# Handing one gate-weight load from SyncE's queue to ScalarE's in a GeGLU feed-forward kernel

## The chip, the core and the metric

The kernel runs on one core of a Trainium2 chip. The metric is the device time of one execution, in microseconds; the kernel before was run six times, and the median is what the change is measured against. One further execution was taken with the hardware profiler. Its trace supplies every duration of a single instruction or transfer below; times inside it are counted in us from the span's start.

## The reference

```python
# x (32, 32, 1024), w_gate and w_up (1024, 3584), w_down (3584, 1024), all bf16
def reference(x, w_gate, w_up, w_down):
    return (gelu_tanh(x @ w_gate) * (x @ w_up)) @ w_down
```

The 32 x 32 rows of x are flattened to 1024 tokens. Two matrix products over the 1024 features give gate and up, each 1024 x 3584; the gated product is multiplied by w_down.

## The kernel before, in words

**Tiles.** Features, 1024 of them, lie in 8 contraction blocks of 128, called k = 0 to 7. The 3584 hidden columns are 28 tiles of 128, called m. Tokens come in two halves of 512. For the first product TensorE holds a 128 x 128 block of a weight matrix and streams 512 tokens of x, with the features on the partitions, so x has to be transposed: `xT[0]` holds half 0, `xT[1]` half 1. The index j is 0 for the gate weights and 1 for the up weights. `first` holds the weights of tiles m = 0 to 3 (512 columns) for both j and all k. It lies in the same SBUF arena as `xT`, so the profile calls all of them `arena`.

**The program.** Every operation is put down with `pr.add(engine, ...)`, which derives its waits from the memory cells that it reads and writes. `finish` sorts the list of each engine but TensorE's by the time given as `at`, and, where that is equal, by the order in which the operations were added. `emit` then writes them out; every instruction therefore shows line 117 in the profile. All loads in the opening have `at=0`, so there the order of adding is the order on each queue. A DMA is issued by the sequencer of SyncE (called SPq in the profile) or of ScalarE (ACTq), and each of the two has a hardware queue of its own: q1 for SyncE, q10 for ScalarE.

**The opening, in the order of the two issuing queues.** First each of them loads half of a small piece of x, blocks k = 0 and 1 of token half 0 (`xn`), which TensorE transposes and DVE copies to `xT[0]`. Blocks k = 2 to 7 of that half are transposed on the way in, by five DMA transposes from SyncE (`load_x`): one each for k = 2, 3, 4 and 5, and a double one for k = 6 and 7. The weights come through `load_first(eng, j, k0, k1)`, 128 KB for one j and one k.

| queue | before: issued in the opening, in order |
| --- | --- |
| SyncE | xn (half), gate k=0, gate k=1, transposes k=2, 3, 4, 5, 6-7 |
| ScalarE | xn (half), up k=0, up k=1, gate k=2, up k=2, gate k=3, up k=3, table load and warm-up Gelu |

Behind that, ScalarE issues four loads of 256 KB that wait for TensorE: gate and up of k = 4-5 after the last matmul of k = 0 (m = 3, j = 1), and gate and up of k = 6-7 after the last matmul of k = 1. SyncE's next load waits for the last matmul of k = 3 (`begin_late`).

**The first stage of matmuls.** After eight warm-up matmuls and the eight transposes of `xn`, TensorE runs `steps`: for each k from 0 to 5, the four tiles m with j = 0 and then the four with j = 1. So 32 matmuls of 128x512 use k = 0 to 3, and the next four need gate k=4, the four after that up k=4. At k = 3 every PSUM bank is copied out into `kept` (ScalarE for even m, DVE for odd m) for later use, and the k = 4 matmul of a bank has to come after that copy. After this stage, TensorE goes on through the rest of the kernel, a Strassen-like scheme over the 2 x 2 blocks of both products, in an order written out by hand.

Of the kernel before, what the change touches and what calls it, by code (L numbers as in the profile page):

```python
# [123 lines left out]
def bass_standalone__geglu_ffn__sampling_kernel(  # L124
# [21 lines left out]
    with ExitStack() as es:  # L146
# [42 lines left out]
        def dma(eng, out, a, at, name, after=()):  # L189
            return pr.add(eng, "dma_start", out, a, at=at, dma=name, after=after)  # L190
# [12 lines left out]
        NX = 2  # L203
# [3 lines left out]
        def load_first(eng, j, k0, k1, after=()):  # L207
            dma(eng, first[:, j, k0:k1, :], w_r[j][:, k0:k1, 0:4 * P], 0, f"w0_{j}_{k0}", after)
# [2 lines left out]
            pr.add("sp", "dma_start_transpose", xT[h][:, k0:k1, :], xf[h * 512:(h + 1) * 512, k0 * P:k1 * P],  # L211
                   dma=f"x{k0}_{h}", after=after)

        for k in range(NX):
            load_first("sp", 0, k, k + 1)
            load_first("act", 1, k, k + 1)
        for k0, k1 in ((2, 3), (3, 4), (4, 5), (5, 6), (6, 8)):
            load_x(0, k0, k1)
        for k in range(2, 4):
# [403 lines left out]
```

## Time and profile before

| | before |
| --- | --- |
| median of 6 runs | 273.14 us (272.87 to 273.6) |
| the profiled execution's own time | 274.18 us |
| its span, first to last instruction | 272.1 us |
| TensorE busy | 268.8 us, 99% of the span |
| DVE, ScalarE, GpSimd busy | 75%, 49%, 14% |
| granted TensorE clock | 1.00 |
| moved by DMA | 27.46 MB, mean 101 GB/s |

How to read it: the profiled execution lies 1.04 us above the median and has 2.1 us around its span, so a difference is worked out within the trace and then put on the median. "Busy" is the time in which an engine has an instruction under way; DMA issue is not counted as busy. A line of the timeline gives start, length, engine, operation, how many were merged, and in brackets the idle time ahead of it and what ended that. "To landing" is the time from the start of the issuing instruction to the last semaphore count of the transfer.

### The profile page before, as it was taken

Reading aid. Unit: us, or ns where it says so; the run is one execution under the profiler, and the core shown is the slowest. Engines: PE = TensorE matmul, PEld = TensorE weight load, DVE = VectorE, ACT = ScalarE, POOL = GpSimd, SP = SyncE. Lnnn points to the kernel's source line nnn. Section 1 sums busy time; section 2 is a strip of 40 time slices with the busy share of each in tenths; the row PEclk is TensorE's granted clock in tenths of the full one; section 3 lists DMA queues with packets and bytes.
Section 4 is the critical chain, followed back from the end, with each engine's and each line's share of the span. In section 5 each row is a group of like instructions: output and inputs, shape, how many; then the busy total and the mean of one; then the engine's idle time right before and its main releaser. Section 6 shows DMA issues by size and latency. Waiting matters only on the chain.

```text
span 272.1 us, 3323 instructions
## 1 busy us (share of the span) xinstructions
PE 268.8 (99%) x1206; PEld 191.6 (70%) x1206; DVE 203.3 (75%) x238; ACT 133.1 (49%) x213; POOL 37.1 (14%) x23
## 2 busy tenths in 40 slices
PE   8999999999999999999999999999999999999996
PEld 3444438888888888888776776674458888888884
DVE  1332997998898889888855738379976999999911
ACT  2335677566756675667455564531220305067452
POOL 1000003033303330333354160000000000000000
PEclk9999999999999999999999999999999999999999
DMA  7999970050393500851900071194010000002102
GB/s 165 235 297 222 285 186 4 1 154 0 94 292 78 148 6 2 255 170 40 272 0 0 0 239 33 60 348 136 0 39 19 4 0 0 0 0 80 58 19 96
DMA packets 47039, 27.46 MB, mean 101 GB/s; under 512 B 8624, under 2 KB 47024, under 8 KB 47024
## 3 DMA queue, kind: packets, MB, share of 16 engines
q1 hardware_dynamic: 44800, 25.30, 34.6%
q10 hardware_dynamic: 2224, 1.97, 3.1%
q8 instruction: 9, 0.15, 0.2%
q14 instruction: 6, 0.05, 0.1%
HBM read 23.33 MB, written 2.10 MB: 93 GB/s over the span
## 4 chain that ended last, share of the span: by engine, by line
PE 97%; DMA 2%; DVE 0%; issue 0%
PE ps L117 97%; DMA arena<-in_w_gate_dram 2%; DVE o L117 0%
## 5 line engine op out<-in xcount | busy, mean ns | idle before, releaser
L117 PE MATMUL ps<-S,T 128*128 128x512 f32 x560 | 129.2, 391 | 0.0
L117 PEld LDWEIGHTS ps<-S,T 128*128 128x128 f32 x560 | 105.1, 188 | 22.4
L117 ACT ACTIVATE tmp<-ps 128x512 f32<-128x512 f32 x64 | 38.1, 597 | 52.8 <-PE ps L117 52.8
L117 POOL TENSOR_TENSOR T<-arena 128x1024 fp32r<-128x1024 bf16 x17 | 36.4, 2152 | 125.4 <-PE ps L117 74.2
L117 PE MATMUL ps<-T,S 128*128 128x512 f32 x224 | 51.3, 390 | 0.0
L117 DVE TENSOR_TENSOR T<-arena,T 128x1024 fp32r<-128x1024 bf16 x42 | 50.9, 1217 | 0.2
L117 DVE TENSOR_TENSOR hT<-tmp,ps 128x512 bf16<-128x512 f32 x56 | 37.1, 684 | 14.9 <-PE ps L117 12.5
L117 PEld LDWEIGHTS ps<-T,S 128*128 128x128 f32 x224 | 42.0, 188 | 8.8
L117 PE MATMUL ps<-arena 128*128 128x512 bf16 x192 | 43.9, 385 | 0.4 <-DMA arena<-in_w_gate_dram 0.3
L117 ACT ACTIVATE ps<-ps 128x512 f32<-128x512 f32 x44 | 25.7, 585 | 36.6 <-PE ps L117 36.6
L117 DVE TENSOR_TENSOR tmp<-ps,tmp 128x512 f32<-128x512 f32 x28 | 19.4, 692 | 24.0 <-PE ps L117 23.8
L117 PEld LDWEIGHTS ps<-arena 128*128 128x128 bf16 x192 | 17.7, 99 | 25.2 <-issue 4.0
L117 DVE TENSOR_TENSOR T<-arena 128x1024 fp32r<-128x1024 bf16 x25 | 30.0, 1220 | 4.4 <-PE ps L117 4.4
L117 PE MATMUL ps<-arena,hT 128*128 128x512 bf16 (+2 forms) x126 | 24.6, 356 | 0.0
L117 DVE TENSOR_TENSOR ps<-ps,tmp 128x512 f32<-128x512 f32 x32 | 22.2, 695 | 3.0 <-PE ps L117 3.0
L117 PEld LDWEIGHTS ps<-arena,hT 128*128 128x128 bf16 x126 | 11.7, 98 | 12.7 <-issue 0.5
L117 ACT ACTIVATE tmp<-tmp 128x512 f32<-128x512 f32 x28 | 17.6, 634 | 2.4 <-DVE tmp L117 2.1
L117 DVE TENSOR_TENSOR S<-hT 128x1024 fp32r<-128x1024 bf16 x14 | 16.6, 1219 | 0.0
L117 ACT ACTIVATE T<-arena 128x1024 fp32r<-128x1024 bf16 x14 | 14.8, 1060 | 0.0
L117 ACT ACTIVATE ps<-hT 128x512 f32<-128x512 f32 x18 | 10.8, 602 | 8.0 <-DVE hT L117 8.0
L117 ACT ACTIVATE hT<-ps 128x512 f32<-128x512 f32 x14 | 8.1, 600 | 11.1 <-PE ps L117 11.1
L117 PE MATMUL ps<-S 128*128 128x512 f32 x56 | 12.9, 389 | 0.0
(32 smaller groups left out, 88.9 us busy)
## 6 DMA issues: line engine op xcount, KB each, us to landing
arena<-in_w_down_dram SPq DMA_DIRECT2D x4, 1792.0 KB, 8.8
arena<-in_w_gate_dram SPq DMA_DIRECT2D x10, 512.0 KB, 4.0
arena<-in_w_up_dram SPq DMA_DIRECT2D x10, 512.0 KB, 5.3
out_dram<-arena SPq DMA_DIRECT2D x12, 128.0 KB, 1.7
arena<-in_w_gate_dram SPq DMA_DIRECT2D x4, 256.0 KB, 4.9
arena<-in_w_up_dram SPq DMA_DIRECT2D x4, 256.0 KB, 5.2
arena<-in_w_up_dram ACTq DMA_DIRECT2D x4, 128.0 KB, 5.2
arena<-in_w_gate_dram ACTq DMA_DIRECT2D x2, 256.0 KB, 5.5
```

What stands on the lines that cost most here:

```text
L117: ins = name(eng, *args, **kw) if callable(name) else getattr(eng, name)(*args, **kw)
```

## The change

The two loads of each of k = 0 and 1 are no longer shared out alternately. SyncE issues gate k=0 alone and then goes on to the transposes. ScalarE issues up k=0, gate k=1 and up k=1, and then what it issued before. Nothing else is touched: the same transfers with the same sizes, destinations and semaphores, the same matmuls in the same order.

| queue | after: issued in the opening, in order |
| --- | --- |
| SyncE | xn (half), gate k=0, transposes k=2, 3, 4, 5, 6-7 |
| ScalarE | xn (half), up k=0, gate k=1, up k=1, gate k=2, up k=2, gate k=3, up k=3, table load and warm-up Gelu |

```diff
-        for k in range(NX):
-            load_first("sp", 0, k, k + 1)
-            load_first("act", 1, k, k + 1)
+        load_first("sp", 0, 0, 1)
+        load_first("act", 1, 0, 1)
+        load_first("act", 0, 1, 2)
+        load_first("act", 1, 1, 2)
         for k0, k1 in ((2, 3), (3, 4), (4, 5), (5, 6), (6, 8)):
             load_x(0, k0, k1)
         for k in range(2, 4):
```

## The prediction, made before the changed kernel was run

> **What bounds the kernel now.** I read the page's busy shares and its chain of waits first, then the chain in order of time, then the timeline of the one place where that chain leaves TensorE, and last the DMA views for that place.
>
> ```profile
> PE 268.8 (99%) x1206; PEld 191.6 (70%) x1206; DVE 203.3 (75%) x238; ACT 133.1 (49%) x213; POOL 37.1 (14%) x23
> ```
>
> TensorE is busy for 268.8 of 272.1 us. The chain that ended last, in order of time, shows where the rest is:
>
> ```profile
> 4.75 2.90 PE ps L117 x9
> 7.65 5.42 DMA arena<-in_w_gate_dram
> 13.07 0.05 issue
> 13.12 256.81 PE ps L117 x1158
> ```
>
> From 13.12 us on it is TensorE alone, to the last output. So whatever the change does must show ahead of that point, and it moves the end one for one. The one DMA on the chain is gate k=4-5, issued by ScalarE at 7.65 as soon as the last matmul of k=0 is over, and landed at 13.07. The timeline there:
>
> ```profile
> 9.37 0.38 ACTq L117 DMA_DIRECT2D arena<-in_w_gate_dram  x1
> 9.78 0.49 ACTq L117 DMA_DIRECT2D arena<-in_w_up_dram  x1
> 11.53 2.48 DVE L117 COPY hT<-ps 128x512 f32<-128x512 f32 x4 [6.50 <-PE ps L117]
> 13.11 0.55 PEld L117 LDWEIGHTS ps<-arena 128*128 128x128 bf16 x4 [0.82 <-DMA arena<-in_w_gate_dram]
> 14.10 7.45 PEld L117 LDWEIGHTS ps<-arena 128*128 128x128 bf16 x36 [0.44 <-DMA arena<-in_w_up_dram]
> ```
>
> The brackets name two late loads: gate k=4 and, four matmuls on, up k=4 (issued at 8.09, landed at 14.06). In the trace the last matmul of k=3 starts at 12.415 and warm matmuls start 0.216 apart, so the next was due at 12.63 and came at 13.12: 0.49 lost. The fifth was due at 13.12 + 4 x 0.22 = 14.00 and came at 14.11: 0.11 lost. The **whole stall is 0.60 us**; nothing after it can be won. Next behind it are DVE's four copies of the k=3 banks, ending at 14.01; without the DMA stall the matmul that needs the last of them would start at 12.63 + 7 x 0.216 = 14.14, so they just fit.
>
> Why are these two loads late? Mean rates by stretch:
>
> ```profile
> core 0: us, PE busy (x) PEld busy (x) DVE busy (x) ACT busy (x) POOL busy (x), PEclk, DMA share, GB/s
> 3.20:4.20 1.00, 1.00 (x9) 0.62 (x8) 0.10 (x1) 0.00 (x0) 0.00 (x0) 1.00 1.13 331
> 4.60:9.50 4.90, 4.85 (x19) 1.99 (x19) 0.43 (x3) 1.12 (x2) 0.00 (x0) 1.00 1.16 182
> 9.50:10.90 1.40, 1.40 (x8) 0.59 (x6) 0.00 (x0) 0.00 (x0) 0.00 (x0) 1.00 1.34 234
> 10.90:12.70 1.80, 1.80 (x9) 0.69 (x7) 1.17 (x2) 1.38 (x3) 0.00 (x0) 1.00 1.23 289
> 12.70:15.00 2.30, 1.97 (x10) 0.73 (x10) 1.32 (x3) 0.69 (x2) 0.00 (x0) 1.00 1.06 301
> ```
>
> The last two columns say it: the 16 DMA engines are full from 3.2 us until long after the stall. In 3.2 to 4.2 both queues carry plain weight rows (331 GB/s). From 4.6 on, when the first transpose packets (256 B) appear beside weights, the same engines move 182. In 9.5 to 10.9 the packets are the transposes' alone: ScalarE's queue has run dry and gate k=4-5, issued at 7.65, has not begun (its first packet stands at 10.92).
>
> **The change part by part.**
>
> *One issue leaves SyncE's queue.* Its two gate issues take 0.92 us for two, so the five transposes, now issued 2.23 to 9.93, go out about 0.47 us earlier, 1.76 to 9.46. SyncE's next load waits for the last matmul of k=3 and goes out at 12.82, so that gap hides the rest. Blocks k=2 and k=3 of x land at 9.01 and 10.58 for matmuls that start at 9.18 and 10.91: they are in time today, so landing earlier is worth nothing by itself.
>
> *One issue enters ScalarE's queue.* Gate k=1 is issued second there, at about 1.80 as against 1.76. The five plain loads behind it (up k=1 to up k=3) go out one slot later, 0.45 to 0.49 us each, and so do the table load (4.23) and the warm-up Gelu, which ends at 5.7 and then at 6.2. Nothing waits on those before 7.65, so this costs nothing; with no gap there, it would be 0.47 us on the critical loads.
>
> *The ladder of weights.* ScalarE's six plain weight loads now land at 4.51, 6.58, 7.22, 8.34, 9.35 and 10.21. Putting the new sequence in these slots, and a seventh one slot (about 1.0) later, against the starts of the matmuls that need them: gate k=1 6.58 for 7.45; up k=1 7.22 for 8.32; gate k=2 8.34 for 9.18; up k=2 9.35 for 10.04; gate k=3 10.21 for 10.91; up k=3 about 11.2 for 11.77. All keep 0.6 us or more, so TensorE's triggers stay at 7.65 and 9.37, and the k=4 loads are issued as now.
>
> *What the engines do with it.* This decides, since the two k=4 loads come behind everything else. The transfers are the same ones, so in the first place their order alone changes. But the transposes start to mix about 0.4 us sooner, as only one 128 KB load is ahead of them on SyncE's queue, and 128 KB of weights leaves the quick plain stretch for the mixed one. 131 kB at 331 GB/s is 0.40 us, at 182 it is 0.72: **+0.32 us**. Were the mixing as quick as in 10.9 to 12.7 (289 GB/s, 0.45 us), it would be +0.06. No row shows seven weight loads beside the transposes, so the ends are wide. Below: the k=4 loads begin when SyncE has issued its last transpose (9.93 now, first packet 10.92) and get all 0.47 us of its head start, and with a quicker mix at most the whole stall, -0.60. Above: gate k=4-5 keeps today's distance to the load ahead of it (13.07 - 10.21 = 2.86) behind one that lands at 11.2, that is 14.07, +1.0. I take +0.32, since 4.6 to 9.5 is the very stretch in which the moved load would travel, while the other two rows stand for a queue that has run dry or a later one.
>
> A rule bears on this. The Trainium skill (Advanced Engine Details and Errata, X-Bar Transpose) says that transposing DMAs are as quick as regular ones on TRN2. By it the mixing costs nothing and this term is 0. The rows disagree, with 182 and 234 GB/s where transposes run and 331 where they don't, and the measurement decides.
>
> A second rule speaks against any gain. DMA: Bandwidth & Descriptors (Issuing engines are not separate DMA queues) says that all issuers share the same 16 engines and that more issuers save only sequencer time. By it alone the change is worth 0, the first rival below; the trace supports it as far as the engines are full from 3.2 us on.
>
> *Sum.* The profiled execution: 274.18 + 0.32 = 274.50. It stood 1.04 above the median, so the median becomes 273.14 + 0.32 = 273.46, given as **273.5 us**. A measurement of this kernel can tell about 0.2%, which is 0.55 us, from no change; the forecast lies inside that, on the slow side.
>
> **The rivals.**
>
> *Only the order changes* (273.1, within 0.2 us). The engines have the same bytes ahead of up k=4 and finish them at the same time. For: the last column is high throughout. Against: the rate differs by half with the mix.
>
> *The head start pays* (272.5 to 272.7). SyncE's queue is through with its transposes 0.47 us sooner, gate k=4-5 begins at 10.45 rather than 10.92, lands at about 12.6, and TensorE goes from k=3 to k=4 without a gap; up k=4 lands at 13.6 for 13.5. It gives 0.47 to 0.60 us. It decides if the dry stretch of ScalarE's queue (9.5 to 10.9) is caused by SyncE's transposes being issued, and is not filled by the seventh load. For: that stretch exists, and its end follows the last transpose issue by 1.0 us. Against: ScalarE's queue is dry only because six loads are through by 9.5; the seventh takes about one slot, 1.0 of those 1.4 us.
>
> *A whole slot is added* (273.8 to 274.3). ScalarE's queue carries 128 KB more and SyncE's less, the engines share by queue, and gate k=4-5 starts a slot later against transposes that no longer leave it room: 13.07 becomes 13.8 to 14.1, and the stall grows by 0.7 to 1.0. It decides once up k=3 lands after about 11.2. For: the critical loads are on the very queue that gets more. Against: the transposes that compete with them begin, and should end, sooner.
>
> One more uncertainty touches all of them: matmuls start 0.43 us apart until 6.8 us and 0.216 from there, while the granted clock reads 1.00. An execution in which that step comes later reaches k=4 later and has less stall, whichever kernel it is.
>
> **How the numbers follow.** The mixing cost (+0.1 to +0.75, about 2 in 5 of it above 0.55): 0.50. Order alone: 0.17. The head start: 0.15, of which 0.10 beyond 0.55. A whole slot: 0.18, all beyond 0.55. Faster: 0.10. Slower: 0.20 + 0.18 = 0.38. Same: 0.30 + 0.17 + 0.05 = 0.52. The range cuts into the head start at 272.6 and into the whole slot at 274.1, leaving out about 1 in 10 on either side. The likeliest case by itself is 273.2 to 273.9.
>
> **What would show it.** In the profile after: transposes issued from about 1.76; a mixed stretch that starts near 4.2 at about 180 GB/s and lasts to about 10 rather than 9.5; gate k=4-5 landing at about 13.4 and up k=4 at about 14.4; TensorE's gap ahead of the 33rd matmul at about 0.8, with everything behind it as long as now. The forecast is wrong if gate k=4-5 lands before 13.0 (head start) or after 13.8 (whole slot), if TensorE stops ahead of k=1, 2 or 3 for a load that slid down the ladder and its triggers move, or if the part after the stall is not 256.8 us long.

## The result

The changed kernel takes 274.68 us in the median of 15 runs (273.57 to 274.94), the kernel before 273.08 us (272.41 to 273.94, 34 runs). The ratio is 1.0051, with a 95% interval of 1.0041 to 1.0061: slower by about 1.4 us. The forecast was 273.5 us with a range up to 274.1. The direction it leaned to was right; the time lies above its range. One later execution of the changed kernel, 278.13 us at a lower granted clock, is left out of every figure below.

The chain in order of time, after (start, length, what):

```profile
4.77 2.61 PE ps L117 x10
7.38 0.03 issue
7.41 6.83 DMA arena<-in_w_up_dram
14.24 0.05 issue
14.28 255.85 PE ps L117 x1154
```

As before, one DMA stands on the chain and everything behind it is TensorE. The DMA is now up k=4-5, issued at 7.41 and landed at 14.24, 6.83 us later; in the kernel before the chain went over gate k=4-5. The timeline of the same stretch, after:

```profile
1.76 8.11 SPq L117 DMA_TRANSPOSE arena<-in_x_dram  x5
5.05 1.28 ACT L117 ACT_TABLE_LOAD   x1 [5.05 <-issue]
6.98 0.40 ACTq L117 DMA_DIRECT2D arena<-in_w_gate_dram  x1
7.41 0.49 ACTq L117 DMA_DIRECT2D arena<-in_w_up_dram  x1
8.57 0.56 PEld L117 LDWEIGHTS ps<-arena 128*128 128x128 bf16 x4 [0.34 <-DMA arena<-in_w_gate_dram]
9.45 0.55 PEld L117 LDWEIGHTS ps<-arena 128*128 128x128 bf16 x4 [0.32 <-DMA arena<-in_w_up_dram]
11.46 0.55 PEld L117 LDWEIGHTS ps<-arena 128*128 128x128 bf16 x4 [0.58 <-DMA arena<-in_w_up_dram]
12.64 0.55 PEld L117 LDWEIGHTS ps<-arena 128*128 128x128 bf16 x4 [0.64 <-DMA arena<-in_w_gate_dram]
14.28 1.63 PEld L117 LDWEIGHTS ps<-arena 128*128 128x128 bf16 x9 [1.09 <-DMA arena<-in_w_up_dram]
```

From up k=1 on, each group of four weight loads is released by a DMA of its own: TensorE follows the weights as they land. By the starts of the matmuls, 0.216 us apart when nothing stops them, it lost less than 0.05 us at each group up to gate k=3, then 0.25 us ahead of up k=3, 0.30 ahead of gate k=4 and 0.76 ahead of up k=4, 1.4 us in all. The rates by stretch, after (the last two columns are the DMA share and GB/s):

```profile
4.60:9.50 4.90, 4.85 (x23) 1.84 (x22) 0.45 (x3) 1.49 (x2) 0.00 (x0) 1.00 1.14 185
9.50:10.90 1.40, 1.40 (x8) 0.57 (x8) 0.00 (x0) 0.14 (x1) 0.00 (x0) 1.00 1.19 170
10.90:12.70 1.80, 1.56 (x8) 0.37 (x6) 1.72 (x3) 1.76 (x4) 0.00 (x0) 1.00 1.17 268
```

The difference to before is in the second line: 170 GB/s where it was 234. There the transposes drained alone, since ScalarE's queue had run dry; now the seventh load (up k=3, last packet at 10.63 rather than 9.46) is still travelling beside them. The transposes' first packet stands 0.73 us earlier than before (3.86 against 4.60), and yet their last one ends later, at 13.38 against 12.66.

And yet the two traces lie only 0.2 us apart in span (272.3 and 272.1), and 0.57 us in time (274.75 and 274.18). The profiled execution of the kernel before was slower than any of the 34 that its median is made of; that of the changed kernel is a usual one. The first experiment goes after this.

### The profile page after: what moved, and what is told of

It reads as the page before. It is cut to its first block, busy times and chain, and to the rows that moved or that the text cites. A ratio compares the mean times of both kernels' runs of the same rounds, so it can differ in the third digit from the quotient of the medians.

```text
span 272.3 us, 3323 instructions
## 1 busy us (share of the span) xinstructions
PE 268.5 (99%) x1206; PEld 191.0 (70%) x1206; DVE 203.4 (75%) x238; ACT 132.9 (49%) x213; POOL 37.2 (14%) x23
## 4 chain that ended last, share of the span: by engine, by line
PE 96%; DMA 3%; DVE 0%; issue 0%
PE ps L117 96%; DMA arena<-in_w_up_dram 3%; DVE o L117 0%
```

## The experiments

Three theories. A: the order of issue; a k=4 load issued behind the double transpose waits for its packets. B: the seventh load on ScalarE's queue makes all behind it late. C: transposes and weights running side by side cost throughput. Differences below are against the kernel before, which had a median of 273.1 to 273.3 in every group of runs. Packet times and counts are counted in the DMA records of each trace, and a packet is put down to a load by its place in the queue's order; the five transposes of half 0 have 3072 packets, the double one 1024 of them.

**The kernel before, once more** (no edit).

> The kernel before, unchanged, for a second trace. The one trace at hand belongs to an execution of 274.18 us, above all the others of this kernel (272.41 to 273.94), with the step in the matmul rate at 6.8 us where the changed kernel's trace has it at 5.5. Theory A (order of issue: a k=4 load that is issued behind the start of the double transpose of k=6-7 waits for most of that transpose): in an execution with the early step both k=4 loads are issued at about 7.0 and 7.4, hardly behind the transpose (7.38), and up k=4 lands at 13.0 or earlier; span about 270.9 us. Theory B (128 KB more on ScalarE's queue, and more of it mixed with transposes): up k=4 lands at about 13.7 and the span is about 271.7, since the bytes ahead of it are the same as in the trace at hand. Time 273.1 us under both.

Measured: 273.10 us, ratio 1.0003 (0.9987 to 1.0019); the profiled execution took 273.41 us with a span of 271.4. Its timeline, and its chain in order of time:

```profile
7.53 0.41 ACTq L117 DMA_DIRECT2D arena<-in_w_gate_dram  x1
7.97 0.49 ACTq L117 DMA_DIRECT2D arena<-in_w_up_dram  x1
13.34 0.36 PEld L117 LDWEIGHTS ps<-arena 128*128 128x128 bf16 x3 [0.29 <-DMA arena<-in_w_up_dram]
```

```profile
4.69 8.20 PE ps L117 x33
12.89 0.05 issue
12.95 10.81 PE ps L117 x49
```

No DMA stands on the chain. The matmul rate steps up at 6.7 us, about as late as in the first trace, but gate and up k=4 land at 11.68 and 13.30 (13.07 and 14.06 there), and TensorE runs through, with up k=4 there 0.08 us ahead of its matmul. So the stall of 0.60 us that the prediction was built on belonged to that execution and is not in every one of this kernel. The step is not what took it away: it came at nearly the same moment, and the k=4 loads were issued only 0.12 us earlier. They landed 1.4 and 0.8 us earlier, so the DMA itself was quicker in this execution. The early step that the expectation spoke of did not come up in this trace.

**The changed kernel, the double transpose held back**, run twice.

```diff
-        for k0, k1 in ((2, 3), (3, 4), (4, 5), (5, 6), (6, 8)):
+        for k0, k1 in ((2, 3), (3, 4), (4, 5), (5, 6)):
             load_x(0, k0, k1)
...
             if (m, j) == (3, 1):
...
+                if k == 1:
+                    load_x(0, 6, 8, [op])
```

> The changed kernel with the double transpose (k=6-7) held back until the last matmul of k=1 is over, so that both k=4 loads are issued ahead of it; the seven weight loads and the four single transposes stay as changed. Theory A: up k=4 lands 1 us or more earlier than 14.24 us, and the time falls from 274.7 to 273.2 or below. Theory B: ScalarE's queue is as long as in the changed kernel, so only the bytes of the double transpose that ran ahead of up k=4 are saved late in the stage; 274.2 to 274.7 us. If holding it makes blocks k=6-7 late (due at about 16.7 us), slower than 274.7 under both.

> The changed kernel with the double transpose held back, a second time, since its first interval (ratio 0.9995 to 1.0033) leaves Theory B's share open. Theory A alone: 272.7 to 273.2 us. With a share of Theory B: 273.5 to 274.0 us, and in the trace TensorE stops ahead of k=2, k=3 or gate k=4 for weight loads that land 0.2 us or more after their matmul was due.

Measured: 273.77 us, ratio 1.0014 (0.9995 to 1.0033), and 273.49 us, 1.0013 (0.9996 to 1.0030). With the changed kernel measured again beside the second of them:

> The changed kernel, unchanged, beside the others on the same chip and for a second trace. Under every theory 274.0 to 274.9 us. Theory A (a k=4 load that is issued behind the start of the double transpose waits for its 1024 packets) expects up k=4's first packet only after at least 2800 of the 3072 transpose packets, with its issue after the double transpose's start at 6.92, and ScalarE's queue dry for 0.7 us or more ahead of it. Theory B (the seventh load on ScalarE's queue makes every later one late) expects up k=3 to land at 11.0 to 11.5 and the k=4 loads to follow without a dry stretch.

Measured: 274.68 us, ratio 1.0042 (1.0020 to 1.0064); up k=4 landed at 14.46, its first packet standing at 12.54 behind 2537 transpose packets, ScalarE's queue dry for 0.5 us ahead of it (0.8 in the first trace of this kernel, behind 2893). That is short of theory A's 2800 packets and 0.7 us; up k=3 landed at 11.41, as theory B had it, but the queue did run dry behind it. Together the changed kernel has a median of 274.68 in 22 runs and with the hold 273.51 in 24: the hold gives back 1.17 us (0.64 to 1.45, resampling both sets). In the first run with the hold the time lay between the two theories' ranges. Rates by stretch and the timeline's weight loads in the first held trace:

```profile
9.50:10.90 1.40, 1.40 (x8) 0.67 (x7) 0.35 (x1) 0.57 (x2) 0.00 (x0) 1.00 1.24 247
11.00:12.50 1.50, 1.45 (x7) 0.50 (x6) 1.50 (x4) 1.39 (x3) 0.00 (x0) 1.00 1.10 344
```

```profile
11.62 0.55 PEld L117 LDWEIGHTS ps<-arena 128*128 128x128 bf16 x4 [0.32 <-DMA arena<-in_w_gate_dram]
12.51 0.33 PEld L117 LDWEIGHTS ps<-arena 128*128 128x128 bf16 x3 [0.34 <-DMA arena<-in_w_up_dram]
```

From 11.0 to 12.5 plain loads have the engines to themselves, up k=4 and behind it gate of k=6-7, at 344 GB/s with 18 transpose packets; up k=4 lands at 12.47 rather than 14.24, hardly ahead of its matmul. Not all of that gap between the traces is the hold's. Gate k=1 landed at 5.45 here and at 6.35 in the changed kernel, ahead of anything that the hold touches, and the two traced executions with the hold took 272.92 and 272.85 us, 0.85 and 0.64 below their medians. The medians are what counts, and by them most of the loss goes when the double transpose is issued later. About 0.4 us stay; in the second trace TensorE stopped 0.29 us ahead of gate k=4, the sign that the second expectation named for theory B.

**The kernel before with the same hold** (the same edit).

> The kernel before with the double transpose held back until the last matmul of k=1, as was done to the changed kernel. With both held, Theory A's wait is absent from both, so held-changed minus held-before is Theory B's share alone. Theory A alone: held-before 272.7 to 273.1 us, and the held changed kernel (273.77) comes down to it when measured again. Theory B has a share: held-before 272.7 to 273.1 and the held changed kernel stays 0.4 to 0.8 us above.

Measured: 273.09 us, ratio 0.9997 (0.9980 to 1.0014). The hold is worth nothing there. In its one trace the step came at 4.7 us, and TensorE stopped 0.7 us ahead of k=2, for the transpose of x, which landed at 8.66. So the double transpose costs time in the changed kernel alone, as far as the medians tell, and held-changed minus held-before, 273.51 - 273.09, leaves 0.42 us (0.06 to 0.99) to the rest of the change.

**The changed kernel with its transposes as late as before.**

```diff
+        dma("sp", pad[:, :], w_r[0][:, 1, 0:2], 0, "pad")
         for k0, k1 in ((2, 3), (3, 4), (4, 5), (5, 6), (6, 8)):
             load_x(0, k0, k1)
```

> The changed kernel with one tiny load (4 bytes on each of 128 partitions, used by nothing) issued by SyncE between gate k=0 and the transposes, so that all transposes go out about 0.45 us later, as in the kernel before, while ScalarE's queue keeps its extra 128 KB. Theory A: the double transpose is issued at about 7.4 us again and most of the loss goes: 273.0 to 273.6 us. Theory B: the extra load and its place on ScalarE's queue stay, so the loss stays: 274.4 to 274.9 us.

`pad` is a buffer that nothing reads; its declaration is left out here. Measured: 273.87 us, ratio 1.0022 (1.0007 to 1.0038), between the two. The seventh load on ScalarE's queue, with the tiny load on SyncE's, costs some 0.6 us by itself, with the transposes issued when they were before. Neither theory's number came out. The traced execution, at 272.73 us, is the quickest of the twelve and waits for no weight load after the first, so it does not show where the 0.6 us lie.

**The other half: gate k=1 by GpSimd's queue**, so that the transposes go early and ScalarE's queue stays as it was.

```diff
-        load_first("act", 0, 1, 2)
+        load_first("pool", 0, 1, 2)
```

> The changed kernel, but gate k=1 is issued by GpSimd's queue. SyncE's transposes go out 0.47 us early as in the changed kernel (the double one at 6.92), while ScalarE's queue has just its six plain loads, as in the kernel before. Theory A (the double transpose is ahead of up k=4, which waits for its packets): the larger part of the loss stays, 273.8 to 274.4 us, with ScalarE's queue dry for 0.7 us or more ahead of up k=4. Theory B (the seventh load on ScalarE's queue): 273.0 to 273.3 us. If gate k=1 by GpSimd lands after 7.4 us, TensorE stops ahead of k=1 for it and the run tells less.

Measured: 273.80 us, ratio 1.0027 (1.0016 to 1.0037). Gate k=1 landed at 6.77 and did not stop TensorE for more than a moment. The stalls, from its timeline:

```profile
9.29 3.61 PE L117 MATMUL ps<-arena 128*128 128x512 bf16 x16 [0.46 <-DMA arena<-in_x_dram]
13.24 0.55 PEld L117 LDWEIGHTS ps<-arena 128*128 128x128 bf16 x4 [0.83 <-DMA arena<-in_w_gate_dram]
14.25 0.76 PEld L117 LDWEIGHTS ps<-arena 128*128 128x128 bf16 x5 [0.46 <-DMA arena<-in_w_up_dram]
```

So this version, with the transposes' head start that was to be the gain of the change, loses 0.7 us by the ratio, about as much as the seventh load by itself. The time is at the lower edge of theory A's range. But half of the stall is not at k=4: by the starts of the matmuls, TensorE lost 0.62 us ahead of k=2, for a transpose of x that was issued early (1.76) and landed at 9.16, and about 0.6 us at k=4. The third queue is a difference of its own here, so how much of the 0.7 us is the head start's is not shown. ScalarE's queue was dry ahead of gate k=4 (10.0 to 11.3), where theory A had it ahead of up k=4.

**Order alone.** Two edits change only when the k=4 loads are issued, or in what order the transposes are.

```diff
 # the kernel before, k=4 loads let go four matmuls later (and no longer after the last matmul of k=0)
+            if (m, j, k) == (3, 0, 1):
+                load_first("act", 0, 4, 6, [op])
+                load_first("act", 1, 4, 6)
 # the kernel before, the last two transposes swapped
-        for k0, k1 in ((2, 3), (3, 4), (4, 5), (5, 6), (6, 8)):
+        for k0, k1 in ((2, 3), (3, 4), (4, 5), (6, 8), (5, 6)):
```

> The kernel before with the two k=4 loads let go four matmuls later (after m=3, j=0 of k=1; about 7.4 to 8.5 us), so that up k=4, and mostly gate k=4 too, is always issued behind the start of the double transpose at 7.38; nothing changes queue. Theory A: ScalarE's queue runs dry for 0.9 us or more ahead of up k=4, which lands at 13.3 to 14.1; 273.9 to 274.7 us. Theory B: the loads' own queue is busy until about 9.3 in any case, so an issue before 8.5 costs nothing; 273.0 to 273.3 us.

> The kernel before with the last two transposes swapped: the double one (k=6-7) is issued at about 6.1 us and the single one of k=5 after it. The weight loads are on the queues of the kernel before. Theory A: both k=4 loads are issued behind the double transpose, their first packets come about 1 us later or more, and the time rises to 274.3 to 275.3 us without any load changing its queue. Theory B: the queues carry the same loads as before and the sum of transpose bytes is the same; 273.0 to 273.4 us.

Measured, later: 273.57 us, ratio 1.0009 (0.9994 to 1.0025). Both k=4 loads were issued behind the double transpose's start (7.88 and 8.35), ScalarE's queue was dry for 1.6 us, and theory A's 0.7 us or more still did not come in the time. When the dry time ended, 2629 of the 3072 transpose packets had started; gate k=4 met the rest and stopped TensorE for 0.55 us, and up k=4 then ran almost clear of them and landed at 13.58. Measured, swapped: 273.55 us, 1.0016 (1.0000 to 1.0031), below theory A's range. In its trace TensorE lost about 0.4 us ahead of gate k=4 and about 1.0 us for k=5 of x; that execution took 274.47 us, 0.9 above the median, so it does not say what the usual one waits for. A missed test.

**The k=4 loads ahead of everything**, issued straight behind up k=3, in both kernels.

```diff
+        load_first("act", 0, 4, 6)
+        load_first("act", 1, 4, 6)
         act(warm[:, 0:1], const0, GELU, 0)
...
-                if k < 2:
-                    load_first("act", 0, 2 * k + 4, 2 * k + 6, [op])
-                    load_first("act", 1, 2 * k + 4, 2 * k + 6)
+                if k == 1:
+                    load_first("act", 0, 6, 8, [op])
+                    load_first("act", 1, 6, 8)
```

> The changed kernel with both k=4 loads issued by ScalarE straight behind up k=3 (at about 5.0 and 5.5 us, ahead of the table load) and not after k=0's last matmul. They are then ahead of the double transpose (6.92) and of k=5's (5.6) in every execution; the seven loads and the early transposes stay. Theory A: 273.2 to 273.8 us, like the kernel with the double transpose held back. Theory B alone: 274.4 to 274.9 us. If x of k=4 or k=5 (due at about 12.6 and 14.2) comes late now, TensorE waits for a transpose in place of a weight load and the gain is smaller.

> The kernel before with both k=4 loads issued straight behind up k=3 (at about 4.2 and 4.7 us). Theory A: up k=4 is ahead of the double transpose (7.38) in every execution, while in the kernel before it is only where the step in the matmul rate comes early; 272.6 to 273.1 us, a little faster than before, with the slowest executions gone. Theory B says nothing on it: 273.2. If the transposes of k=2 or k=3, which now have more weights beside them, land after 9.2 or 10.9, slower than before.

Measured: changed 274.20 us, ratio 1.0027 (1.0012 to 1.0043); before 274.18 us, 1.0037 (1.0022 to 1.0052). Both lie outside the ranges of both theories. Being ahead in the order does not bring theory A's gain, and the kernel before loses 1 us by it. The rate and, from the timeline, the stall in the changed one:

```profile
11.00:14.70 3.70, 2.72 (x12) 0.84 (x12) 2.55 (x4) 2.07 (x4) 0.00 (x0) 1.00 1.19 251
```

```profile
14.38 1.63 PEld L117 LDWEIGHTS ps<-arena 128*128 128x128 bf16 x9 [1.19 <-DMA arena<-in_w_up_dram]
```

In this stretch 1535 transpose packets went by. In the queue's order, the packets of the two k=4 loads went from 10.3 to 13.4, with 652 transpose packets among them; in the held kernel they went from 9.7 to 11.8, with 224. In the kernel before, up k=4 landed at 12.62, in time, and it was k=4 of x that came late (12.92). Theory A falls as it was put. What fits these runs is that it matters not who is issued first, but whether transposes are still travelling when the k=4 loads are.

**Weights first, transposes after.** SyncE waits with its first transpose until a weight load has landed.

```diff
+            load_x(0, k0, k1, [loads[1]] if k0 == 2 else ())
```

Here `loads` holds the four loads of k = 2 and 3 in ScalarE's order, now put down ahead of the transposes: `loads[1]` is up k=2. The third version waits for `loads[0]`, gate k=2.

> The kernel before, but SyncE issues its first transpose (k=2) only once up k=2 has landed, so that the plain weight loads run first and the transposes after them. Theory C (transposes running beside weight loads move fewer bytes in all, and the changed kernel has more of that): apart, the weights of k=1 to 3 have landed by 6.5 us and the transposes follow at 234 to 285 GB/s, blocks k=2 to 5 landing at about 7.4, 8.7, 10 and 11.2; no stall is left but for a late k=2, and the slowest executions go: 272.6 to 273.1 us. If C is wrong, every transpose is late by the 3 us that it was held, TensorE stops ahead of k=2, and the time is 274 us or more.

> The changed kernel with the same: the first transpose waits until up k=2 has landed. The weights keep the changed kernel's queues, seven of them on ScalarE's. Theory B (the seventh load on ScalarE's queue is what costs, whatever runs beside it): 273.7 us or more, 0.5 and more above the kernel before held apart. Theory C (it costs only by running beside transposes): within 0.3 us of the kernel before held apart, 272.6 to 273.3, with the seven loads landed by 6.9 us. Theory A (order ahead of up k=4) is met by both, since the double transpose goes out after 10 us.

> The kernel before with the first transpose let go one load earlier, when gate k=2 has landed (about 0.5 us sooner). Theory C: k=2 lands 0.5 us sooner than with the wait for up k=2, at the price of some mixing with the last three plain loads; 272.6 to 273.1 us, the better of the two if k=2 is what TensorE waits for. If C is wrong: 274 us or more.

Measured: before, waiting for up k=2, 279.28 us, ratio 1.0218 (1.0199 to 1.0238); changed, 278.11 us, 1.0195 (1.0158 to 1.0232); before, waiting for gate k=2, 277.00 us, 1.0151 (1.0114 to 1.0187). All miss theory C's times by 4 to 6 us; what the expectations gave for C being wrong, 274 us or more with TensorE stopped ahead of k=2, is what came. TensorE's timeline and the rates of the first of the three (the third column from the right is the granted clock):

```profile
12.55 17.71 PE L117 MATMUL ps<-arena 128*128 128x512 bf16 x70 [4.32 <-DMA arena<-in_x_dram]
```

```profile
4.90:7.10 2.20, 2.20 (x12) 1.01 (x11) 0.00 (x0) 0.80 (x2) 0.00 (x0) 1.00 0.76 256
8.40:14.20 5.80, 1.65 (x4) 0.59 (x5) 0.00 (x0) 0.00 (x0) 0.00 (x0) 0.69 1.17 230
14.20:15.60 1.40, 1.40 (x5) 0.56 (x4) 0.00 (x0) 0.00 (x0) 0.00 (x0) 0.50 1.28 272
```

Half of the forecast held: without transposes beside them all weights up to k=3 were there at 7.5 us. But the k=4 to 7 loads, let go by TensorE at 6.5 and 8.3, then ran beside the transposes, and k=2 of x, whose packets were through at 10.1, counted as landed at 12.42 only. The weights were ahead and x was late. So these versions are no clean test either. The two placements differ by 1.2 us the other way round here, beside stalls of 4 to 5 us for x, so theories B and C are not told apart by them. No version tried beats the kernel before: the held one equals it.

## Why the prediction was wrong

*Where to look* was right: only the first 14 us move, and the rest follows one for one (255.85 us of TensorE behind 14.28, 256.81 behind 13.12, with four more matmuls to the left of it, 1154 against 1158).

*The issues* began as worked out: transposes from 1.76, gate k=1 at 1.80. They did not end so: the double transpose took 2.95 us to issue rather than 2.55, and the last issue was over at 9.87, not 9.46, so the head start had shrunk from 0.47 to 0.06 us. The last two plain loads on ScalarE took 0.61 and 0.64 us to issue rather than 0.45, and nothing in the trace waited for that.

*The ladder* was close in its landings (forecast 6.58, 7.22, 8.34, 9.35, 10.21 and 11.2; measured 6.35, 7.64, 8.43, 9.41, 10.29 and 11.41) and wrong in "all keep 0.6 us or more". The due times came from an execution in which matmuls were slow until 6.8 us. In the trace after, they are quick from 5.5 on, and every due time is nearly 0.7 us earlier (the last matmul of k=0 starts at 6.57 rather than 7.24). From up k=1 on TensorE has next to no slack at any rung, and at up k=3 it loses 0.25 us. The triggers moved with it, from 7.65 and 9.37 to 6.98 and 8.76, which the prediction had named as a sign of being wrong.

*The base* is the first step that failed: "so the median becomes 273.14 + 0.32" carried a stall of 0.60 us over to executions that need not have it. The second trace of the kernel before has none. The changed kernel waited for up k=4 in both its traces (landed at 14.24 and 14.46, with the step at 5.5 and 4.8). Against the first trace the change cost 0.57 us in the profiled times, where the forecast had 0.32; that it comes so near is in part chance, since it sets an execution above all others of its kernel against a usual one. Against the median it costs 1.4 to 1.6. The prediction named another uncertainty, the moment of the step, and thought that it "touches all of them". Whether an early step helps the kernel before more than the changed one is not shown: no trace of the kernel before has one, and in two of its variants, with the step at 4.7 and 5.5, TensorE stopped 0.7 and 0.3 us ahead of k=2 for x.

*The mixing cost* is the term that was mis-sized: +0.32 us by one load's bytes at two rates. What it left out is that the load fills the very stretch in which the transposes drained alone, so that they end later though they begin earlier (13.38 and 13.99 in two traces of the changed kernel, 12.66 and 12.02 in two of the kernel before), and up k=4 meets what is left of them. By the hold, that meeting is 1.17 us; 0.42 (0.06 to 0.99) remain, and whether these are the 0.32 of the forecast is not shown. The prediction's signs pointed both ways. Gate k=4-5 landed at 12.60, ahead of the 13.0 that was to mean a head start that pays, and the kernel was slower all the same, through up k=4. The rival of the whole slot named another, up k=3 landing after about 11.2; it landed at 11.41, and the time came out 0.4 us above that rival's. But its path was not this one either, since it had gate k=4-5 at 13.8 to 14.1.

On the rules. The Trainium skill (Advanced Engine Details and Errata, X-Bar Transpose) has transposing DMAs as quick as regular ones; here transposes alone moved 234 GB/s (9.5 to 10.9 in the trace before) and 285 (12.0 to 12.75 in the trace after), weights alone 344, and both together 170 to 185 in the changed kernel up to 10.9. The company alone does not set that rate: in the kernel before, 507 transpose packets and 240 weight rows side by side moved 313 GB/s from 10.95 to 12.15, and the changed kernel with the hold 247 from 9.5 to 10.9. What makes the early stretch slow is not shown. The rows, of the trace after and of the trace before:

```profile
12.00:12.75 0.75, 0.60 (x4) 0.11 (x3) 0.75 (x2) 0.75 (x2) 0.00 (x0) 1.00 1.26 285
10.95:12.15 1.20, 1.20 (x7) 0.54 (x6) 0.62 (x2) 0.83 (x2) 0.00 (x0) 1.00 1.14 313
```

The second rule of the prediction, by which the change is worth nothing, did not hold here either: the same transfers in another share between the queues cost 1.4 us. And on the phase of the step: the page TensorE: Matmul & The Clock Gate (What's actually happening) says that the window which releases the clock runs freely, so the moment differs between executions. The traces agree that it does, with the step at 6.8 and 6.7 us in two of the kernel before, 5.5 and 4.8 in two of the changed kernel, and ahead of the first weight matmul (4.7) in the held one. The clock records of the two traces of the kernel before begin, at 1.00, at 6.75 and 6.59, just ahead of the step; for the time before that they hold none, so the 1.00 that the prediction set against the slow matmuls was not a reading.

*Left open*: how the remaining 0.4 us divides between the seventh load and the earlier transposes (each half alone costs 0.6 to 0.7, with intervals that reach 0.2 and 1.0), and why the same loads run faster in some executions: with the pad, up k=3 was through at 8.4 us in its one trace, in the changed kernel at 10.6, and the k=4 loads of the kernel before landed 1.4 and 0.8 us apart in its two traces.

## What to carry to other kernels

Before sizing a stall from one trace, set that execution's time beside the spread of the others: if it is the slowest, its stall may not be there in the median, and a change after which the usual execution stalls costs all of it. The same holds for the traces of the experiments. Moving a load from one busy queue to another was not neutral here: ask what drained while the second queue was dry, and who meets it now. What gave time back here was to hold back the transpose that is due last; sending the urgent loads earlier did not help, and holding back all transposes cost 4 to 6 us. In the kernel that had no such loss, the hold was worth nothing.

## What the runs showed of the hardware that was not expected

In one stretch, 9.5 to 10.9 us, the changed kernel's engines moved 170 GB/s with transposes and weight rows side by side, and the kernel before 234 with transposes alone; elsewhere both kinds together reached 313. A transpose counts as landed well behind its packets: with the transposes held back until up k=2 had landed, those of k=2 were through at 10.1 us and the landing stands at 12.42; it was 7.4 and 9.0 in the first trace before, 6.5 and 8.5 in that after. For the two k=4 weight loads of those two traces the distance was 0.6 to 0.8 us. And in the version that stopped TensorE for 4.3 us, from 8.2 to 12.55, the granted clock fell to 0.50 at 10.55, while TensorE stood, and stayed there for 6.8 us (line 14.20:15.60 above); until 17.4 the matmuls started 0.43 us apart again, so a stall of that length is paid a second time. Two stops of 1.9 us, in the version that let the transpose go earlier, left the clock at 1.00.
